# Partial sums of the up products held in PSUM, and the two plain down products of batches 2 to 7 split into quarters

## The chip, the cores and the metric

The kernel runs on one core of a Trainium2 chip. The metric is the device time of one execution in microseconds. TensorE (PE, with PEld for its weight loads) multiplies matrices, VectorE (DVE) does elementwise work, ScalarE (ACT) does activation functions and copies, and SyncE (SP) issues the transfers between the main memory and the on-chip memory. TensorE writes its results to PSUM, from where VectorE or ScalarE fetch them. All data here are 32-bit floats; a float32 matrix product of the program stands in the trace as two records of the same shape.

## What is computed

The reference, cut to what matters:

```python
# x: (8, 8, 512, 64), state: (8, 8, 32, 64)
a  = softmax(scale * x @ state.T);  xread = a  @ state
a2 = softmax(scale * state @ x.T);  sread = a2 @ x
rows = concat([xread, sread], axis=2)      # to (8 * 544, 512)
h = rows @ w_in                            # 512 -> 2048
g = h * (1.0 / (1.0 + exp(-1.702 * h)))
out = g @ w_out                            # 2048 -> 512
```

The 512 rows of x of each of the 8 batches go through both large products, and at the very end the 32 state rows of all batches together ("sr").

The kernel replaces the usual 8 products of 2x2 blocks by 7 (the Strassen-Winograd scheme): with A and B split into 2x2 blocks,

```
S1 = A21 + A22   S2 = S1 - A11   S3 = A11 - A21   S4 = A12 - S2
T1 = B12 - B11   T2 = B22 - T1   T3 = B22 - B12   T4 = B21 - T2
P1 = A11 B11  P2 = A12 B21  P3 = S4 B22  P4 = A22 T4  P5 = S1 T1  P6 = S2 T2  P7 = S3 T3
U2 = P1 + P6   C11 = P1 + P2   C12 = U2 + P5 + P3
C21 = U2 + P7 + P4             C22 = U2 + P7 + P5
```

(In the code the names of the parts are those of the kernel.)

## The kernel before

The first product ("up", rows @ w_in, with the softmax's product folded in) is done per block of features u, in seven products of 4 records each. PSUM banks hold x, y and z; VectorE adds what is in a bank to what it has already put into the on-chip memory (c21, c12, c22), and ScalarE takes the result through the activation function:

```python
def begin(u):
    nc.scalar.copy(c21, product(u, "x", l11, b11, True))
    add(product(u, "y", m2, t2, True), c21, c12)
def middle(u):
    z = product(u, "z", m1, t1, True)
    gelu(c11, product(u, "x", l12, b21, False))      # goes on summing in the bank
    add(product(u, "y", l21, t3, False), c21, c22)
    add(z, c22, c22)
    gelu(c22, c22)
def end(u):
    add(product(u, "y", l22, t4, False), c21, c21)
    gelu(c21, c21)
    add(product(u, "z", m4, b22, False), c12, c12)
    gelu(c12, c12)
    ...
    if u: s12(b, u - 1, ntok)                         # S1, S2 of the second product
for u in range(NU):                                   # NU = 4
    begin(u)
    if u: end(u - 1)
    middle(u)
    ...
def rest():
    end(NU - 1)
    s12(b, NU - 1, ntok)
    for u in range(NU): s3(b, u, ntok)
```

`add` is one VectorE instruction of 512 columns. `rest` runs inside the second product, after the first half of P1 ("P1a" below). The second product ("down", g @ w_out) is also done in seven products P1 to P7. Five of them (P3 to P7) are split again, into seven products of quarters, each of 8 records of 128x128. P1 and P2 are plain: 32 records each of 128x256:

```python
product(bank(0), A_of(0, 0), B11, "P1")
nc.scalar.copy(k1, bank(0))
...
sums_of((S1, r), (S2, (q1, q2, q4)))                  # sums for P5 and P6
third_of(S1)
product(bank(1), A_of(0, 1), B21, "P2")
tt(osb, bank(1), k1)
out(0, 0, osb)
hook("P2")
...                                                   # P5, P6, P3, P7, P4, each by strassen_low
```

The split form, with three banks x, y, z and `at(i)` for work of other parts that is put between the products:

```python
def strassen_low(left, right, bank, R, at):
    product(x, a11, b11, True);   nc.scalar.copy(p, x);    at(1)
    product(y, s2, t2, True);     add(u2, y, p);           at(2)
    product(x, a12, b21, False);  nc.scalar.copy(c11, x);  at(3)
    product(z, s1, t1, True);     add(c22, z, p);          at(4)
    product(y, a21, t3, False);   add(c22, y, c22);        at(5)
    product(z, s4, b22, False);   add(c12, z, u2);         at(6)
    product(y, a22, t4, False);   add(c21, y, p);          at(7)
```

(Summing goes on in one bank with `False`: after `u2` has been read, the fifth product lands on top of the second.) The sums s1, s2, s4 and the third (in place of a21) of the left side are made by VectorE before or during the product that stands ahead; those of the right side (t1, t2, t4) are kept outside and loaded, 768 KB each time (`low_load(k, i)`), into one of two places.

Attention work of the next batch hangs on named places in this sequence (`turn_x` ahead of the second product, then at "P1a" the state, at "P2a" the scores, the matrices M 0 and 1, and the maxima; later the exponentials, sums, transposes, and M 2 and 3). Each engine works through its own instructions strictly in the program's order (the program is scheduled by hand).

Of the kernel before, what the change touches and what calls it, by code (L numbers as in the profile page):

```python
# [10 lines left out]
FP32 = mybir.dt.float32  # L11
# [3 lines left out]
ALU = mybir.AluOpType  # L15
# [5 lines left out]
def kernel(  # L21
# [30 lines left out]
    nc = tc.nc  # L52
# [39 lines left out]
    def att_ps(shape, name):  # L92
        return psA.tile(shape, FP32, tag="att", name=name)
# [356 lines left out]

    def att_M(b, c, spare=False):

        m = mpool.tile([P, NG, FC], FP32, tag=f"M{turns['M'] % NFC if b < 2 else c}", name=f"M_{b}_{c}")
        turns["M"] += 1
        A[b]["M", c] = m
        name = f"M_{b}_{c}_"
        ps = [psH.tile([P, FC], FP32, tag="h", name=name + str(g)) if spare else att_ps([P, FC], name + str(g)) for g in range(NG)]
        by_state(b, ps, lambda rows, j: w_in[c][rows, j])
        for g in range(NG):
            nc.scalar.copy(m[:, g], ps[g])  # L460
# [177 lines left out]

    outside = {k: dram.tile([P, 3 * FC], FP32, name=f"low_{k}") for k in range(2, 7)}
    turn_rooms = [low[:, 3 * i : 3 * i + 3].rearrange("p k n -> p (k n)") for i in range(2)]  # L640
# [38 lines left out]

    def strassen_low(left, right, bank, R, at):  # L680

        b11, t3, b21, b22, t1, t2, t4 = right
        a11, a12, a21, a22, s1, s2, s4 = left
        p, u2 = (pu[:, i] for i in range(2))
        x, y, z = (v[:, :P] for v in bank)

        def product(ps, lhs, rhs, first):
            for f in range(QF):
                nc.tensor.matmul(  # L689
                    ps, lhs[f], rhs[:, f], start=(first and f == 0), stop=(f == QF - 1), skip_group_check=True  # L690
                )

        def add(out, x0, x1):
            nc.vector.tensor_tensor(out=out, in0=x0, in1=x1, op=ALU.add)

        c11, c12, c21, c22 = (R[:, i, P * k : P * (k + 1)] for i in range(2) for k in range(2))
        product(x, a11, b11, True)
        nc.scalar.copy(p, x)
        at(1)
        product(y, s2, t2, True)  # L700
        add(u2, y, p)
        at(2)
        product(x, a12, b21, False)
        nc.scalar.copy(c11, x)
        at(3)
        product(z, s1, t1, True)
        add(c22, z, p)
        at(4)
        product(y, a21, t3, False)
        add(c22, y, c22)  # L710
        at(5)
        product(z, s4, b22, False)
        add(c12, z, u2)
        at(6)
        product(y, a22, t4, False)
        add(c21, y, p)
        at(7)

    def strassen_two(key, dst, hooks, a4):
# [63 lines left out]

        product(bank(0), A_of(0, 0), B11, "P1")
        nc.scalar.copy(k1, bank(0))
        *r, p5 = spare_M()
        r = [v.rearrange("p (k h t) -> p k h t", k=2, h=2) for v in r]
        p5 = p5.rearrange("p (r n) -> p r n", r=2)
        sums_of((S1, r), (S2, (q1, q2, q4)))
        third_of(S1)  # L790
        product(bank(1), A_of(0, 1), B21, "P2")
        osb = opool.tile([P, 2, HN], FP32, tag="osb", name=f"osb_{key}_00")
        tt(osb, bank(1), k1)
        out(0, 0, osb)
# [20 lines left out]

        def sums(y, rooms):


            r1, r2, r4 = rooms

            def parts(k, i):
                return [y(2 * k + f // 2, i)[:, f % 2] for f in range(QF)]

            def both(fn):
                def step():
                    for u in range(NU // 2):
                        fn(u)

                return step

            return [
                both(lambda u: tt(r1[:, u], y(u, 1), y(2 + u, 1))),
                both(lambda u: tt(r2[:, u], r1[:, u], y(u, 0), ALU.subtract)),
                both(lambda u: tt(y(u, 1), y(u, 0), y(u, 1), ALU.subtract)),
                both(lambda u: tt(r4[:, u], y(2 + u, 0), r2[:, u], ALU.subtract)),
            ], (parts(0, 0), parts(1, 0), parts(0, 1), parts(1, 1), *(blocks(v) for v in rooms))

        def lowly(name, left, right, kept, banks, R, own):
            def at(i):
                for fn in own.get(i, ()):  # L840
                    fn()
                hook(f"{name}.{i}")

            b11, t3, b21, b22 = halves_of(right)
            strassen_low(left, (b11, t3, b21, b22, *kept), banks, R, at)

        def y_of(u0, o):
            return lambda u, i: g[u0 + u][:, :, o + P * i : o + P * (i + 1)]

        steps3, left3 = sums(y_of(0, half), (v1, v2, v4))  # L850
# [14 lines left out]
        lowly("P3", left12, B22, low_b, [h0, h1, o], p3, own3)  # L865
        if key + 1 < B:
            low_load(5, 1)
        hook("run")
# [5 lines left out]
        lowly("P7", left3, T3, low_a, [o, h0, h1], k3, {k + 1: steps4[k : k + 1] for k in range(4)})  # L874
        if key + 1 < B:
            low_load(2, 0)
        osb = opool.tile([P, 2, HN], FP32, tag="osb", name=f"osb_{key}_11")
# [16 lines left out]
    def hooks_next(b):  # L894
# [5 lines left out]

        at("P1a", att_state, b)
        at("P2a", att_scores, b)

        at("P2a", load_x, b)
        at("P2a", att_M, b, 0)
        at("P2a", att_M, b, 1, True)
        at("P2a", att_blocks, b)
        at("P2a", att_s_max, b)
        at("P2a", att_s_exp, b)
        at("P2a", eT_out, b)  # L910
        at("P2a", x_max, b, 0)
        at("P2a", x_sub, b, 0)
        at("P5.1", x_exp, b, 0)
# [117 lines left out]
    def up_strassen(b, ntok, left, right, between=(), beside=()):  # L1031
# [4 lines left out]
        b11, b21, b22, t1, t2, t3, t4 = right  # L1036
        banks = {}

        def product(u, bank, lhs, rhs, first):
            if first:  # L1040
                if bank == "x":
                    banks[bank, u] = psH.tile([P, 2, QT], FP32, tag="h", name=f"upx_{b}_{u}")
                else:
                    o = bank_o[2 * (u % 2) + (bank == "z")]
                    banks[bank, u] = o[:, : 2 * QT].rearrange("p (k t) -> p k t", k=2)
            ps = banks[bank, u]
            n = len(lhs)
            for k in range(2):
                o = 2 * P * (u % 2) + P * k
                for i in range(n):  # L1050
# [3 lines left out]
                    )  # L1054
            return ps

        def gelu(dst, src):
            nc.scalar.activation(out=dst, in_=src, func=AF.Gelu_apprx_sigmoid)  # L1058

        def add(ps, x, dst):  # L1060
            nc.vector.tensor_tensor(out=dst, in0=ps, in1=x, op=ALU.add)  # L1061

        def aside():
            if beside:
                fn, args = beside.pop(0)
                fn(*args)


        def begin(u):
            l11, l12, l21, l22, m1, m2, m4 = left(u)  # L1070
            G[b, u], G[b, NU + u] = free.pop(0), free.pop(0)
            _, c12 = quarters(b, u, ntok)
            c21, _ = quarters(b, NU + u, ntok)
            nc.scalar.copy(c21, product(u, "x", l11, b11, True))
            add(product(u, "y", m2, t2, True), c21, c12)
            aside()

        def middle(u):
            l11, l12, l21, l22, m1, m2, m4 = left(u)
            c11, c12 = quarters(b, u, ntok)  # L1080
            c21, c22 = quarters(b, NU + u, ntok)
            z = product(u, "z", m1, t1, True)
            gelu(c11, product(u, "x", l12, b21, False))
            add(product(u, "y", l21, t3, False), c21, c22)
            add(z, c22, c22)
            gelu(c22, c22)
            aside()

        def end(u):
            l11, l12, l21, l22, m1, m2, m4 = left(u)  # L1090
            c11, c12 = quarters(b, u, ntok)
            c21, c22 = quarters(b, NU + u, ntok)
            add(product(u, "y", l22, t4, False), c21, c21)
            gelu(c21, c21)
            add(product(u, "z", m4, b22, False), c12, c12)
            gelu(c12, c12)
            aside()
            if u:
                s12(b, u - 1, ntok)

        for u in range(NU):
            begin(u)
            if u:
                end(u - 1)
            middle(u)
            for fn, args in between[u] if u in between else ():
                fn(*args)

        def rest():
            end(NU - 1)  # L1110
            s12(b, NU - 1, ntok)
            for u in range(NU):
                s3(b, u, ntok)

# [153 lines left out]
    for b in range(1, B):  # L1268
        if b > 1:
            ahead = {"P1a": [(up_strassen(b, S, *parts_x(b), A[b]["sums"]), ())]}  # L1270
        else:
# [7 lines left out]
        else:  # L1279
# [6 lines left out]
            hooks["P3.7"] = [(low_third, (T1,))]  # L1286
            beside = steps[10:16] + [(low_third, (t,)) for t in (T2, T3, T4, B22)]
            ahead["P1a"][:0] = [steps[i] for i in (0, 1, 4, 5)]
        for name, first in ahead.items():
# [45 lines left out]
```

## Time and profile before

| | |
|---|---|
| time, median of three runs | 708.77 us (708.74 to 708.86) |
| span of the profiled execution | 706.9 us |
| ScalarE: copies out of PSUM on the line of `begin` (L1074), 512 columns | 24, mean 573 ns |
| ScalarE: activation on PSUM (L1058), 512 columns | 24, mean 597 ns |
| VectorE: s12's two lines (L565, L566), 512 columns | 28 each, mean 683 and 692 ns |
| VectorE: additions of 128 columns in the split products (L694), largest group | 42, mean 281 ns |
| share of the 16 transfer engines | 42.3% |
| loads of right-hand sums (low), 256 KB | 78, 3.8 us to landing |

The busy time of an engine counts the time in which at least one of its instructions is under way; instructions of one engine overlap a little, so a group's mean is longer than the distance from one start to the next. A line of the chain gives the start and the length of a piece of work that was on the path to the end. In the timeline, what stands in brackets is the idle time of that engine ahead of the instruction, and what ended it.

### The profile page before, as it was taken

The page shows a single profiled execution, that of the slowest core. Times are in us where ns is not written, and L with a number is a line of the kernel's source. Part 1 is how long each engine was busy: PE and PEld are TensorE (multiplying, and loading weights), DVE is VectorE, ACT ScalarE, POOL GpSimd, SP SyncE. Part 2 cuts the span into 40 slices and gives each one's busy share as a digit, 9 for nine tenths or more (in the row PEclk, how much of TensorE's full clock was granted, in tenths as well). Part 3 has the DMA queues.
Part 4 walks back from the last instruction along what each step waited for, and adds up shares of the span by engine and source line. Part 5 has one row for each costly group of instructions (what it writes and reads, how often), then busy time and mean ns, then how long its engine had stood idle before and what let it go on. Part 6 is the DMA issues. An engine that isn't in the chain of part 4 may idle for free.

```text
span 706.9 us, 12667 instructions
## 1 busy us (share of the span) xinstructions
PE 694.9 (98%) x4973; PEld 558.1 (79%) x4975; DVE 602.4 (85%) x1246; ACT 230.8 (33%) x456; POOL 0.8 (0%) x8
## 2 busy tenths in 40 slices
PE   8989999999999999999999999999999999999996
PEld 3433544458998799879988899889987998899995
DVE  6999799999978998799978996899789987888650
ACT  5686520014224413433243423342243124200210
POOL 0000000000000000000000000000000000000000
PEclk9999999999999999999999999999999999999999
DMA  8921246228742384309550765047432940041001
GB/s 230 368 74 54 93 146 154 115 89 206 213 118 37 61 194 145 69 9 206 148 105 1 152 182 120 16 82 199 137 51 48 194 148 16 0 125 57 16 1 29
DMA packets 143914, 77.89 MB, mean 110 GB/s; under 512 B 113904, under 2 KB 127728, under 8 KB 143856
## 3 DMA queue, kind: packets, MB, share of 16 engines
q1 hardware_dynamic: 143856, 77.09, 42.3%
q8 instruction: 39, 0.64, 0.4%
q14 instruction: 19, 0.16, 0.1%
HBM read 61.08 MB, written 15.99 MB: 109 GB/s over the span
## 4 chain that ended last, share of the span: by engine, by line
PE 95%; ACT 2%; DMA 2%; SPq 0%; DVE 0%; issue 0%; DVEq 0%
PE low L689 21%; PE o L1051 17%; PE o L738 14%; PE o L689 10%; PE o L542 8%; PE h L524 7%; PE upx L1051 6%; PE M L320 4%; PE o L585 2%; PE o L320 1%; PE sr L500 1%; PE warm L125 1%; PE upx_sr L1051 1%; DMA out_dram<-osb_sr 1%; DMA xn<-in_x_dram 1%; ACT low L219 1%
## 5 line engine op out<-in xcount | busy, mean ns | idle before, releaser
L1061 DVE TENSOR_TENSOR g<-o,g 128x512 f32<-128x512 f32 (+1 forms) x140 | 88.0, 650 | 51.1 <-PE o L1051 50.1
L738 PE MATMUL o<-w_out,g 128*128 128x256 f32 x448 | 100.6, 381 | 0.0
L738 PEld LDWEIGHTS o<-w_out,g 128*128 128x128 f32 x448 | 84.4, 190 | 16.6 <-issue 5.5
L1058 ACT ACTIVATE g<-g 128x512 f32<-128x512 f32 (+1 forms) x84 | 49.8, 600 | 100.9 <-DVE g L1061 100.9
L1051 PE MATMUL upx<-aT,M 128*128 128x256 f32 x192 | 49.3, 379 | 0.0
L1051 PE MATMUL o<-ta,M 128*128 128x256 f32 x192 | 49.3, 379 | 0.0
L1051 PE MATMUL o<-ta,ms 128*128 128x256 f32 x192 | 48.3, 379 | 0.0
L689 PE MATMUL low<-low,g 128*128 128x128 f32 x336 | 44.4, 275 | 0.0
L689 PEld LDWEIGHTS low<-low,g 128*128 128x128 f32 x336 | 40.9, 192 | 0.0
L460 ACT COPY M<-M 128x512 f32<-128x512 f32 x64 | 33.1, 598 | 22.7 <-PE M L320 22.7
L1051 PEld LDWEIGHTS o<-ta,ms 128*128 128x128 f32 x192 | 36.6, 190 | 4.9
L1051 PEld LDWEIGHTS o<-ta,M 128*128 128x128 f32 x192 | 36.6, 190 | 4.9
L1051 PEld LDWEIGHTS upx<-aT,M 128*128 128x128 f32 x192 | 36.1, 191 | 4.6
L689 PE MATMUL low<-sums,later 128*128 128x128 f32 x280 | 37.0, 275 | 0.0
L689 PEld LDWEIGHTS low<-sums,later 128*128 128x128 f32 x280 | 34.6, 192 | 0.4
L320 PE MATMUL M<-w_in,stT 64*32 64x512 f32 x512 | 31.9, 594 | 0.0
L527 ACT ACTIVATE g<-h 128x512 f32<-128x512 f32 x24 | 14.0, 591 | 54.7 <-PE h L524 54.7
L524 PE MATMUL h<-low,M 128*128 128x512 f32 x64 | 29.6, 597 | 1.5 <-DVE low L408 1.5
L524 PE MATMUL h<-aT,M 128*128 128x512 f32 x64 | 28.7, 599 | 1.4 <-ACT M L460 1.4
L689 PE MATMUL low<-w_out,g 128*128 128x128 f32 x224 | 29.6, 275 | 0.0
L542 PE MATMUL o<-w_out,g 128*128 128x512 f32 x64 | 28.6, 594 | 0.0
L542 PE MATMUL o<-w_out,sums 128*128 128x512 f32 x64 | 28.3, 593 | 0.0
(210 smaller groups left out, 1295.2 us busy)
## 6 DMA issues: line engine op xcount, KB each, us to landing
low<-low SPq DMA_DIRECT2D x78, 256.0 KB, 3.8
later<-in_moe_w_out_dram SPq DMA_DIRECT2D x16, 512.0 KB, 3.6
xn<-in_x_dram SPq DMA_DIRECT2D x28, 256.0 KB, 4.8
low<-low SPq DMA_DIRECT2D x9, 768.0 KB, 4.0
w_out<-in_moe_w_in_dram SPq DMA_DIRECT2D x12, 512.0 KB
xsq<-in_x_dram SPq DMA_DIRECT2D x96, 64.0 KB, 2.3
out_dram<-osb SPq DMA_DIRECT2D x18, 256.0 KB, 3.1
out_dram<-later SPq DMA_DIRECT2D x14, 256.0 KB, 2.2
```

What stands on the lines that cost most here:

```text
L125: nc.tensor.matmul(ps, zeros[:, :P], zeros, start=True, stop=True)
L320: nc.tensor.matmul(ps[g][st], A[b]["stT"][rows, st], rhs(rows, j), start=True, stop=True)
L460: nc.scalar.copy(m[:, g], ps[g])
L524: nc.tensor.matmul(hps, lhs[i], rhs[i], start=(i == 0), stop=(i == n - 1))
L527: nc.scalar.activation(out=G[key, f // 2][:, f % 2, :ntok], in_=hps, func=AF.Gelu_apprx_sigmoid)
L542: nc.tensor.matmul(ops, G[key, f // 2][:, f % 2, P * r : P * (r + 1)], w_out[:, f], start=(f == 0), stop=(f == NF - 1))
L585: nc.tensor.matmul(ps[:, r], lhs[f][:, P * r : P * (r + 1)], rhs[:, f], start=(first and r == 0 and f == 0), stop=(f == HF - 1), skip_grou ...
L689: nc.tensor.matmul(ps, lhs[f], rhs[:, f], start=(first and f == 0), stop=(f == QF - 1), skip_group_check=True)
L738: nc.tensor.matmul(ps[:, r], lhs[f][:, P * r : P * (r + 1)], rhs[:, f], start=(r == 0 and f == 0), stop=(f == HF - 1), skip_group_check=True,)
L1051: nc.tensor.matmul(ps[:, k], lhs[i][:, o : o + P], rhs[i], start=(first and k == 0 and i == 0), stop=(i == n - 1), skip_group_check=True,)
L1058: nc.scalar.activation(out=dst, in_=src, func=AF.Gelu_apprx_sigmoid)
L1061: nc.vector.tensor_tensor(out=dst, in0=ps, in1=x, op=ALU.add)
```

## The change

It has two parts. First, the sums of the up products are left in PSUM: ScalarE copies the first product x into the bank y beforehand (a seed), so that the next products sum on top of it, and one of the two other sums is written by VectorE into a bank z, on which again a product sums. VectorE then adds twice in each u, where it added five times; ScalarE copies three times, where it copied once. The activation reads the banks. `s12` and `s3` of the block before are done among the up products. Second, P1 and P2 of the batches 2 to 7 become seven products of quarters too, as P3 to P7 are; batch 1 keeps the plain ones. The aim is less work on TensorE (7 of 8 quarter products in P1 and P2), with room on VectorE made by the first part. For it the right-hand sums of B11 and B21 are made in batch 1 and kept outside, and two more loads take place in each batch. What hung on "P1a" and "P2a" moves.

The core of the diff, with cuts marked:

```diff
@@ strassen_low
-        product(x, a11, b11, True)
...
+        def q1(): product(x, a11, b11, True);   nc.scalar.copy(p, x)
+        def q2(): product(x, a12, b21, False);  nc.scalar.copy(c11, x)
+        def q6(): product(y, s2, t2, True);     add(u2, y, p)
+        def q5(): product(z, s1, t1, True);     add(c22, z, p)
+        def q7(): product(y, a21, t3, False);   add(c22, y, c22)
+        def q3(): product(z, s4, b22, False);   add(c12, z, u2)
+        def q4(): product(y, a22, t4, False);   add(c21, y, p)
+        for i, q in enumerate((q1, q5, q2, q6, q7, q3, q4) if late else (q1, q6, q2, q5, q7, q3, q4)):
+            q()
+            at(i + 1)
@@ strassen_two
-        product(bank(0), A_of(0, 0), B11, "P1")
-        nc.scalar.copy(k1, bank(0))
+        if key == 1:
+            product(bank(0), A_of(0, 0), B11, "P1")
+            nc.scalar.copy(k1, bank(0))
+        else:
...
+            for fn in steps1:                      # 8 instructions of 256 columns
+                fn()
+            o, h0, h1 = low_banks()
+            lowly("P1", left1, B11, low_b, [h0, o, h1], p1, {}, True)
+            nc.scalar.copy(k1, p1)
+            low_load(5, 1)
...
+            for fn in steps2:                      # 8 more
+                fn()
+            hook("P1")
...
-        sums_of((S1, r), (S2, (q1, q2, q4)))
-        third_of(S1)
-        product(bank(1), A_of(0, 1), B21, "P2")
-        tt(osb, bank(1), k1)
+        if key == 1:
...
+        else:
+            o, h0, h1 = low_banks()
+            own2 = {2: [lambda: sums_of((S1, r))], 4: [lambda: third_of(S1)], 5: [lambda: sums_of((S2, (q1, q2, q4)))]}
+            lowly("P2", left2, B21, low_a, [h0, o, h1], osb, own2, True)
+            low_load(2, 0)
+            tt(osb, osb, k1)
@@ strassen_two, after P3 (and alike after P7, with B21 and place 0)
-        if key + 1 < B:
-            low_load(5, 1)
+        if key == 1:
+            low_made(0, B11, 1)
+            low_third(B11)
+        elif key + 1 < B:
+            low_load(0, 1)
@@ hooks_next
+        p1, p2 = ("P1a", "P2a") if first else ("P1.2", "P1")
+        at(p1, att_state, b)
+        at(p2, att_scores, b)
...
+        at("P2a" if first else "P2", x_max, b, 0)
+        at("P2a" if first else "P2", x_sub, b, 0)
@@ up_strassen
+        first_x(0); seed(0); first_w(0)            # seed: nc.scalar.copy(Y(u), X[u])
+        for u in range(NU):
...
+            if u + 1 < NU: first_x(u + 1)
+            product(Y(u), u, m2, t2)
+            nc.scalar.copy(c12, Y(u))
+            add(Z(u), W[u], c12)
+            aside()
+            if u: last_y(u - 1)                    # product(Y, l22, t4), gelu
+            if u + 1 < NU: seed(u + 1)
+            product(X[u], u, l12, b21)
+            gelu(c11, X[u])
+            if u: sums_after(u - 1)                # s12, s3
+            product(Y(u), u, l21, t3)
+            nc.scalar.copy(c22, Y(u))
+            add(c22, W[u], c22)
+            gelu(c22, c22)
+            aside()
+            if u + 1 < NU: first_w(u + 1)
+            product(Z(u), u, m4, b22)
+            gelu(c12, Z(u))
...
+        def rest():
+            last_y(NU - 1)
+            sums_after(NU - 1)
@@ the loop over the batches
-            ahead = {"P1a": [(up_strassen(b, S, *parts_x(b), A[b]["sums"]), ())]}
+            ahead = {"P1.1": [(up_strassen(b, S, *parts_x(b), A[b]["sums"]), ())]}
...
-            beside = steps[10:16] + [(low_third, (t,)) for t in (T2, T3, T4, B22)]
+            beside = steps[10:16] + [(low_third, (t,)) for t in (B11, B21, T2, T3, T4, B22)]
-            ahead["P1a"][:0] = [steps[i] for i in (0, 1, 4, 5)]
+            ahead["P1.2"] = [steps[i] for i in (0, 1, 4, 5)]
```

## The prediction

> **What bounds the kernel now.** I read the page first (busy time and chain), then one batch cut out of the steady part by its period, then the timeline of that batch, which gives the cost of single instructions. The page:
>
> ```profile
> PE 694.9 (98%) x4973; PEld 558.1 (79%) x4975; DVE 602.4 (85%) x1246; ACT 230.8 (33%) x456; POOL 0.8 (0%) x8
> ...
> PE 95%; ACT 2%; DMA 2%; SPq 0%; DVE 0%; issue 0%; DVEq 0%
> ...
> L1061 DVE TENSOR_TENSOR g<-o,g 128x512 f32<-128x512 f32 (+1 forms) x140 | 88.0, 650 | 51.1 <-PE o L1051 50.1
> L738 PE MATMUL o<-w_out,g 128*128 128x256 f32 x448 | 100.6, 381 | 0.0
> ```
>
> TensorE sets the end: 95% of the chain. But VectorE, at 85%, has little to spare, and an average hides where. The chain in order of time repeats every 75.63 us (281.08, 356.71, 432.34, always the first up product of a batch). So I cut the batch 356.71 to 432.34 into stretches; the columns are length, then busy time of PE, PEld, DVE, ACT, POOL, then granted clock, DMA share and GB/s:
>
> ```profile
> 356.71:380.00 23.29, 23.29 (x109) 20.55 (x109) 17.34 (x28) 11.45 (x19) 0.00 (x0) 1.00 0.32 60
> 380.00:392.20 12.20, 12.20 (x89) 9.54 (x94) 11.46 (x20) 2.41 (x5) 0.00 (x0) 1.00 0.00 0
> 392.20:397.00 4.80, 4.80 (x43) 3.56 (x28) 4.70 (x11) 4.51 (x8) 0.00 (x0) 1.00 1.02 198
> 397.00:410.00 13.00, 13.00 (x118) 13.00 (x118) 12.61 (x34) 2.49 (x8) 0.00 (x0) 1.00 0.91 187
> 410.00:421.00 11.00, 11.00 (x168) 9.50 (x168) 10.93 (x30) 3.49 (x10) 0.00 (x0) 1.00 0.63 200
> 421.00:432.34 11.34, 11.34 (x99) 11.24 (x99) 9.37 (x24) 0.85 (x4) 0.00 (x0) 1.00 0.41 117
> ```
>
> See two things. TensorE has no gap anywhere. VectorE is idle for 6 us in the first stretch (the up products) and for 2 us in the last; from 380 to 421 it works 39.7 of 41 us. TensorE runs just ahead of a VectorE that is full there.
>
> The cost of one instruction must be its start-to-start distance, not its "mean ns", which overlaps with its neighbour. From the timeline:
>
> ```profile
> 355.68 1.03 PE L1051 MATMUL upx<-aT,M 128*128 128x256 f32 x4
> ...
> 356.74 0.58 ACT L1074 COPY g<-upx 128x512 f32<-128x512 f32 x1 [4.17 <-PE upx L1051]
> ...
> 379.66 2.48 DVE L156 STREAM_TRANSPOSE xsq<-xsq 128x512 f32<-128x512 f32 x4
> ...
> 389.18 0.69 DVE L745 TENSOR_TENSOR spare_M<-later 128x512 f32<-128x512 f32 x1
> 389.78 0.68 DVE L745 TENSOR_TENSOR g<-later 128x512 f32<-128x512 f32 x1
> ...
> 398.50 1.06 PE L689 MATMUL low<-sums,later 128*128 128x128 f32 x8
> 398.77 0.29 DVE L694 TENSOR_TENSOR pu<-low,pu 128x128 f32<-128x128 f32 x1
> 398.98 0.68 DVE L745 TENSOR_TENSOR g<-g,later 128x512 f32<-128x512 f32 x1
> ...
> 416.00 0.75 DVE L745 TENSOR_TENSOR later<-g,g 128x256 f32<-128x256 f32 x2
> 416.67 0.75 DVE L745 TENSOR_TENSOR later<-later,g 128x256 f32<-128x256 f32 x2
> ```
>
> VectorE: 0.60 us for 512 columns (389.18 to 389.78; about 0.71 where it needs the result just before it), 0.335 for 256 (two in 0.67), 0.20 for 128. TensorE: an up product of 4 records takes 0.862 (16 such records of 128x256 on L738 take 3.45 us in the chain), a quarter product of 8 records 0.894. From the start of an up product to the ScalarE copy that reads it: 1.06 us, so 0.20 after the next product has begun. A copy of 512 columns is done after 0.58.
>
> [...] a product that accumulates onto a bank waits until VectorE has read it; in the built program each such matmul waits for a VectorE semaphore. No line of the trace before shows that wait lasting, since it is always met there.
>
> **The change part by part.**
> TensorE: P1 and P2 of batches 2 to 7 were 64 records by 0.2156 = 13.80 us a batch; they become 14 quarter products by 0.894 = 12.52. Saved 1.29 us a batch, 7.7 in six.
> VectorE, up products: five additions per u become two; 12 fewer in a batch, by 0.60 = 7.2 us less. ScalarE gets 8 more copies, about 4.6 us, of a time in which it is half idle.
> VectorE, P1 and P2: each gets 8 sums of 256 columns (2.68) and 5 additions (1.0), together 7.4 us more.
> So VectorE's total hardly changes. But the 7.2 leave the stretch where it was idle, and the 7.4 enter the stretch where it was full. In exchange seven instructions of the late part go: two additions of the last up products, and s12 of one u and s3 of three, now done among the up products; 7 x 0.60 = 4.2 us. Some 3.2 us net are added where VectorE was full, and the dependences make it worse. I walk through one batch (2 to 6), t = 0 at the first up product, in the order in which the built program has each engine's instructions:
>
> - Up: 27 products, then the first product of P1 at 23.3. By the walk no wait: the copies between two products of one bank are ready 0.1 us or more ahead.
> - The last c22 is copied after the product that ends at 22.43: 22.64 + 0.58 = 23.2; its addition to 23.9. Then VectorE turns x of the next batch, 4 x 0.60: to 26.25. Only then the first sum of P1: both halves done at 27.0.
> - TensorE has nothing but P1's first product (to 24.2) and the last up product (to 25.05). The second product of P1 needs that sum: it starts near 26.7. **Wait 1.7.**
> - VectorE: sums to 28.9, s12 and s3 of the last u to 30.9, then P1's two additions, done 31.35. The fifth product accumulates onto the bank that the second of them reads, and stands straight after the product that filled it. TensorE is there at 29.6: **wait 1.8.**
> - The additions of P1's last three products each follow TensorE, so VectorE is mostly idle until 34.5. Then P2's sums (2.7), two transposes and the maxima of the scores (2.8), one addition, three sums for P5 (2.0): P2's like addition is done at 42.5. TensorE has the scores, M and four products, to 40.4: **wait 2.1.**
> - In P5 the same pattern behind x_max, x_sub and s4: **0.45 and 0.6.** In P6 VectorE is just in time again.
>
> Sum 6.6, less 1.3: a batch longer by 5.3 us; five batches 26.6. Batch 7 turns no x, but its four sums for the state rows stand between P1's additions: waits 3.7 and 2.0, less 1.3, 4.4. Batch 1 keeps its plain products and makes the sums of B11 and B21: 8 instructions by 0.62, 5 us in a VectorE that was full (410 to 421 in its own batch's copy), less the 1.6 us that it idles in P4: about 3. The third sums undone before the state rows cost 2 x 0.6 where VectorE has room. 708.8 + 26.6 + 4.4 + 3 = 742.8.
>
> **The rivals.**
> (1) TensorE stays the only bound: 708.8 - 7.7 = 701. For it: TensorE's share and the unchanged VectorE total. Against: 380 to 421 above. A version of it with only the unavoidable gap (product, addition, next product on one bank, some 0.6 us in P1 and in P2 each) would be 708.8 - 7.7 + 7 = 708.
> (2) ScalarE's new copies stop TensorE among the up products: 8 hand-offs a batch, the tightest about 0.1 us early. If each lost 0.2 us: 1.6 a batch, 10 us in all; alone 711, with my waits 750. Against: ScalarE has 11.5 busy of 23.3 us there.
> (3) A transfer is late: two more loads of 768 KB in a batch, and P5's and P6's sums are now loaded after P1 and P2, where the DMA share is 0.91 to 1.02. By the walk they have 8 us and more, and pieces of 256 KB land in 3.8. Late by 1 us a batch it would add 6.
>
> **Range and chances.** The waits come from orders that are fixed and durations that repeat, so their sign is fairly sure; each is good to some 0.3 us, five of them in six batches to some 9 us all the same way. If half of them were hidden by something I overlooked, 725; with rivals 2 or 3 on top, 755. Slower by over 2% means over 723. Predicted 743, range 727 to 755; faster by over 2% 0.01 (even rival 1 gives 1.1%), within 2% 0.09, slower 0.90.
>
> **What would show it.** Right: the batch takes near 81 us; TensorE's waits are for VectorE on the quarter products of P1 and P2, and gone from P6 on; the stretch of the up products has none; VectorE idles about 3 us in the second half of P1. Wrong: a period near 74.3 (rival 1), TensorE waits for ScalarE at up products (2) or for a load (3), or sums of 256 columns much under 0.33 us.

## The result, and the profile after

The changed kernel takes 757.98 us (median; 756.88 to 760.5), the kernel before 708.77: a ratio of 1.070, 95% interval 1.068 to 1.072. Predicted were 743, range 727 to 755. The direction and the kind of cost were right; the size was 15 us short.

The page of the changed kernel, the same lines as before (busy time by engine, the granted clock in 40 slices, the chain by engine):

```profile
PE 705.7 (93%) x5261; PEld 569.3 (75%) x5263; DVE 603.7 (80%) x1328; ACT 263.6 (35%) x536; POOL 0.8 (0%) x8
...
PEclk9999999999999999999999999999999999899999
...
PE 69%; DVE 17%; ACT 6%; DMA 3%; issue 3%; SPq 0%; DVEq 0%; ACTq 0%
```

VectorE's busy time has hardly moved (602.4 to 603.7), as worked out. Yet the chain, 95% TensorE before, now runs through VectorE for 17% and through ScalarE for 6%. So the same amount of VectorE's work stands at worse places. PE's busy time has gone up (694.9 to 705.7) although there is less to multiply: in part because some products ran at a lower clock (0.50 in the stretches shown below), which the slice with an 8 in the row of the clock hints at (c1 below, whose clock drops only at the very end, has 697.5).

TensorE's waits in the whole span (total, times, longest):

```profile
PE o L691 <- DVE pu L696: 15.6, 12, 3.5
PE low L691 <- ACT pu L702: 11.2, 5, 2.2
```

The first line was predicted. The second, five waits of 2.2 us for a ScalarE copy, was not. One batch, which begins at 457.19 and lasts 82.71 us (75.63 before), shows where both stand. From TensorE's timeline (start, length; in brackets the idle time and what ended it):

```profile
484.09 1.13 PE L691 MATMUL low<-low,spare_M 128*128 128x128 f32 x8 [1.53 <-issue]
...
488.72 1.16 PE L691 MATMUL o<-w_out,g 128*128 128x128 f32 x8 [1.61 <-DVE pu L696]
...
498.65 1.16 PE L691 MATMUL low<-w_out,g 128*128 128x128 f32 x8 [2.25 <-ACT pu L702]
...
501.23 1.16 PE L691 MATMUL o<-w_out,left 128*128 128x128 f32 x8 [0.53 <-DVE pu L696]
...
508.14 1.16 PE L691 MATMUL low<-sums,later 128*128 128x128 f32 x8 [0.17 <-DVE pu L696]
509.67 1.16 PE L691 MATMUL o<-sums,spare_M 128*128 128x128 f32 x8 [0.37 <-DVE spare_M L696]
```

The lines are P1's second and fifth product, P2's third and fifth, and two of P5. Besides the wait, see the length: a quarter product right after a wait shows 1.13 to 1.16, most others 1.06. It ends up to 0.1 us later; with the six waits here and smaller ones not shown, that is some 0.9 us in a batch more than before.

For P1's second product this profile names no releaser (`issue`). VectorE's timeline has the turn of x, and behind it the sum that the product multiplies, up to the moment when it starts; in the profile of a4 below, where the same five waits occur, they are put down to that line:

```profile
481.20 2.48 DVE L156 STREAM_TRANSPOSE xsq<-xsq 128x512 f32<-128x512 f32 x4
483.61 0.71 DVE L758 TENSOR_TENSOR spare_M<-g,g 128x256 f32<-128x256 f32 x2
...
PE low L691 <- DVE spare_M L758: 7.9, 5, 1.6
```

Why P2's third product waits for ScalarE is in ScalarE's own timeline:

```profile
495.07 0.62 ACT L462 COPY M<-o 128x512 f32<-128x512 f32 x1
495.70 1.28 ACT L372 ACT_TABLE_LOAD   x1
497.00 0.69 ACT L372 ACTIVATE e<-o,mx 128x512 f32<-128x512 f32 x1
...
497.68 0.68 ACT L372 ACTIVATE e<-o,mx 128x512 f32<-128x512 f32 x1
...
498.34 0.26 ACT L702 COPY pu<-low 128x128 f32<-128x128 f32 x1
```

P2's third product accumulates onto the bank of its first, and must wait until ScalarE has copied that first product out. TensorE finished it near 495.3; but ScalarE has its instructions in order, and ahead of the copy stand the last copy of M, a table load of 1.28 us and the two exponentials of the scores. The copy runs 3 us late. (The first exponential starts 0.02 us after the end of the load, at 497.00 after 496.98.)

Last, the clock. Stretches of 3.41 us (length, busy time of PE, PEld, DVE, ACT, POOL, granted clock, DMA share, GB/s), two pairs with a drop and, between them, the two stretches over which P2's wait of 2.25 us in the batch at 457.19 is spread:

```profile
329.93:333.34 3.41, 1.34 (x12) 1.34 (x13) 2.15 (x6) 2.15 (x7) 0.00 (x0) 1.00 0.90 144
333.34:336.75 3.41, 3.03 (x15) 2.73 (x14) 1.84 (x4) 0.12 (x1) 0.00 (x0) 0.50 0.96 142
...
493.77:497.18 3.41, 2.63 (x32) 1.89 (x16) 3.38 (x8) 3.38 (x6) 0.00 (x0) 1.00 1.06 213
497.18:500.59 3.41, 1.94 (x16) 1.86 (x16) 2.12 (x6) 1.69 (x6) 0.00 (x0) 1.00 0.86 139
...
579.10:582.51 3.41, 1.17 (x11) 1.15 (x11) 2.12 (x7) 2.19 (x6) 0.00 (x0) 1.00 0.90 167
582.51:585.92 3.41, 3.03 (x15) 2.73 (x14) 2.03 (x4) 0.27 (x1) 0.00 (x0) 0.50 0.96 143
```

After P2's wait in the batches at 290.54 and 539.90 the granted clock is 0.50 for 3.41 us, and those two batches take 83.94 us where the other three take 82.71. In the last batch three such stretches are at 0.50, two of them in a row (654.2 to 661.0, and 667.9 to 671.3).

### The profile page after: what moved, and what is told of

The parts are those of the page before. It is cut to its first block, busy times and chain, and to the rows that moved or that the text cites. A ratio compares the mean times of both kernels' runs of the same rounds, so it can differ in the third digit from the quotient of the medians.

```text
span 757.2 us, 13522 instructions
## 1 busy us (share of the span) xinstructions
PE 705.7 (93%) x5261; PEld 569.3 (75%) x5263; DVE 603.7 (80%) x1328; ACT 263.6 (35%) x536; POOL 0.8 (0%) x8
## 4 chain that ended last, share of the span: by engine, by line
PE 69%; DVE 17%; ACT 6%; DMA 3%; issue 3%; SPq 0%; DVEq 0%; ACTq 0%
PE low L691 16%; PE o L691 11%; PE o L1113 11%; PE o L544 7%; PE h L526 7%; PE upx L1113 5%; DVE g L758 3%; PE M L320 3%; DVE spare_M L758 3%; PE o L587 2%; PE upw L1113 2%; DVE xsq L156 2%; ACT M L462 1%; ACT e L372 1%; DMA out_dram<-osb 1%
## 5 line engine op out<-in xcount | busy, mean ns | idle before, releaser
L691 PE MATMUL low<-w_out,g 128*128 128x128 f32 x416 | 56.2, 278 | 12.2 <-ACT pu L702 11.2
L691 PEld LDWEIGHTS low<-w_out,g 128*128 128x128 f32 x416 | 51.3, 192 | 17.8 <-ACT pu L702 12.2
L702 ACT COPY pu<-low 128x128 f32<-128x128 f32 x33 | 8.7, 264 | 97.7 <-PE low L691 65.2
L462 ACT COPY M<-M 128x512 f32<-128x512 f32 x59 | 30.7, 595 | 14.4 <-PE M L320 14.4
L1119 ACT ACTIVATE g<-o 128x512 f32<-128x512 f32 (+1 forms) x56 | 31.3, 559 | 10.7 <-PE o L1113 10.7
L691 PE MATMUL o<-w_out,g 128*128 128x128 f32 x160 | 23.3, 290 | 11.5 <-DVE pu L696 11.5
L691 PEld LDWEIGHTS o<-w_out,g 128*128 128x128 f32 x160 | 20.2, 198 | 17.7 <-DVE pu L696 12.6
L1122 DVE TENSOR_TENSOR o<-upw,g 128x512 f32<-128x512 f32 x18 | 12.6, 700 | 24.0 <-ACT g L1159 24.0
L1113 PE MATMUL o<-ta,ms 128*128 128x256 f32 x120 | 30.8, 379 | 0.0
L691 PE MATMUL low<-low,spare_M 128*128 128x128 f32 x160 | 22.0, 280 | 7.7 <-issue 6.1
```

The lines of the kernel that those rows point to most:

```text
L691: nc.tensor.matmul(ps, lhs[f], rhs[:, f], start=(first and f == 0), stop=(f == QF - 1), skip_group_check=True)
L1113: nc.tensor.matmul(ps[:, k], lhs[i][:, o : o + P], rhs[i], start=(first and k == 0 and i == 0), stop=(i == n - 1), skip_group_check=True,)
L1122: nc.vector.tensor_tensor(out=out, in0=ps, in1=x, op=ALU.add)
```

## The experiments

All times are medians; ratios are to the kernel before on the same chip (708.8).

**a1, part 1 alone.** The sums of the up products in PSUM, with P1 and P2 left as they were.

```diff
-            ahead = {"P1.1": [(up_strassen(b, S, *parts_x(b), A[b]["sums"]), ())]}
+            ahead = {"P1a": [(up_strassen(b, S, *parts_x(b), A[b]["sums"]), ())]}
...
-        if key == 1:
+        if True:
...
```

(`if key == 1` kept the plain P1 and P2 to batch 1.)

> Only the first part of the change: sums of the up products in PSUM; P1 and P2 stay plain in all batches, with no extra loads. Theory (the wait is made by VectorE's full queue in P1 and P2): 706 to 710 us, no wait of TensorE among the up products, VectorE about 7 us a batch lighter. Rival (the hand-offs through seeded banks stop TensorE): over 715 us, with waits of TensorE for ScalarE on the up products.

Measured: 709.55, ratio 1.0010 (1.0003 to 1.0017). VectorE's busy time falls from 602.4 to 551.3 and ScalarE's rises from 230.8 to 257.7, and nothing comes of it: TensorE was the bound among the up products before and still is. Rival 2 of the prediction (hand-offs from ScalarE stop the up products) falls.

**a2, part 2 alone.** The quarters in P1 and P2, with the old up products. The third sums of P1 overwrite blocks that the old order reads later, so other numbers come out; the instructions are the same.

```diff
-    def up_strassen(...):   # the changed one
+    def up_strassen(...):   # that of the kernel before
```

> Only the second part: the up products as before (five additions a u on VectorE, s12 and s3 late), P1 and P2 of batches 2 to 7 in quarters. Theory: the 7.4 us of VectorE's work a batch enter the full stretch without the 4.2 us that the first part takes out of it, so it is slower still than the change: 775 to 790 us. Rival (the first part is what hurts): 701 to 715 us.

Measured: 792.04, ratio 1.117 (1.115 to 1.120), 2 us above the range. P1's fifth product alone waits 5.9 us in a batch, and runs at half the clock afterwards (0.50 from 507.54 to 514.36 us; 2.08 instead of 1.06 to 1.16):

```profile
510.63 2.08 PE L691 MATMUL o<-w_out,g 128*128 128x128 f32 x8 [5.93 <-DVE pu L696]
```

So part 1 is what makes room for part 2: worth nothing alone, it takes 34 us off what part 2 costs. The room does not suffice.

**a3, without the sums of the left operands.** The 16 sums a batch that P1 and P2 need are left out and raw blocks multiplied in their place; the output is another.

```diff
-            for fn in steps1:
-                fn()
...
+            left1 = raw(y_of(0, 0))
...
-            for fn in steps2:
-                fn()
+            left2 = raw(y_of(NU, 0))
```

> The change with the 16 sums of 256 columns a batch left out (the products of P1 and P2 read the plain quarters in their place, so this part of the computation is missing), all products and their additions kept. Theory: 5.4 us less on VectorE in the full stretch; waits of about 0.9, 1.0 and 0.5 us stay, and the granted clock stays at 1.00: 718 to 730 us. Rival 1 (waits between adjacent products of one bank): 745 or more. Rival 2 (late loads): 755 or more, unchanged.

Measured: 741.52, ratio 1.046 (1.044 to 1.048): above the range by 11. P1's first wait is gone, but P2's third product waits for ScalarE exactly as long as before (2.25), and the clock drops to 0.50 after it in three of the five batches instead of two:

```profile
488.22 1.67 PE L691 MATMUL low<-w_out,g 128*128 128x128 f32 x8 [2.25 <-ACT pu L702]
489.69 1.91 PE L691 MATMUL o<-low,g 128*128 128x128 f32 x8
```

With 32 us less of VectorE's busy time this wait has not moved: that fits ScalarE's order, as the timeline above suggested; b2 below changes this order itself.

**a4, without the two added loads.** Two loads of right operands a batch are left out; the output is another.

```diff
-        elif key + 1 < B:
-            low_load(0, 1)
...
-        elif key + 1 < B:
-            low_load(1, 0)
```

> The change with the two additional loads of right-hand sums left out in batches 2 to 6 (P1 and P2 then multiply by sums of other products that lie there, so the values are others; the instructions of the engines are the same). Theory: 755 to 760 us, unchanged. Rival (transfers come late or crowd): at least 6 us less.

Measured: 756.54, ratio 1.067 (1.065 to 1.070). A batch without a drop of the clock takes 82.70 (82.71 with the loads), so the loads cost nothing that shows; the 1.4 us lie within the spread of the executions. Rival 3 falls.

**b1, the turn of x among the up products.**

```diff
-            if b > 1:
-                turn_x(b + 1)
...
-            ahead = {"P1.1": [(up_strassen(b, S, *parts_x(b), A[b]["sums"]), ())]}
+            ahead = {"P1.1": [(up_strassen(b, S, *parts_x(b), {**A[b]["sums"], **({2: [(turn_x, (b + 1,))]} if b + 1 < B else {})}), ())]}
```

> The changed kernel, with the turn of x of the next batch (4 x 0.60 us of VectorE) moved from P1's first product to the up products, where VectorE has about 1.95 us of slack in each batch. Theory (VectorE's order: at P1 the turn stands ahead of the sum that TensorE waits for): the two waits of P1, 1.7 and 1.8 us together, shrink to about 1.0, so about 2.45 us in each of five batches, some 12 in all: 740 to 748. Rival (VectorE has as much work as before, so the wait only moves to a later product or into the up products): 756 to 760.

Measured: 751.11, ratio 1.059 (1.057 to 1.061); outside the range, though P1 did what the theory said: the wait before its second product is gone, the one before its fifth is 1.49 (product to product). A batch without a drop of the clock now takes 80.65, some 2.06 less than 82.71; five of those are 10 us. But there is just one such batch; in the next four P2's wait falls so that the clock drops each time, and they take 82.01 to 82.23:

```profile
406.82:410.23 3.41, 1.17 (x10) 0.98 (x10) 2.15 (x7) 3.05 (x7) 0.00 (x0) 1.00 1.26 218
410.23:413.64 3.41, 3.29 (x16) 2.99 (x15) 2.06 (x4) 0.27 (x1) 0.00 (x0) 0.50 0.73 109
488.74:492.15 3.41, 1.17 (x10) 0.97 (x10) 2.15 (x6) 3.15 (x7) 0.00 (x0) 1.00 1.25 225
492.15:495.56 3.41, 3.41 (x16) 3.17 (x16) 2.07 (x4) 0.27 (x1) 0.00 (x0) 0.50 0.74 111
```

81.92 us lie between the two drops, 24 times 3.413, as between any two neighbours of the four from 328.31 to 574.07 us: the batch has come into step with the points at which the clock drops, and so meets one each time.

**b2, the exponentials behind P2's first copy.**

```diff
-        at(p2, att_s_exp, b)
-        at(p2, eT_out, b)
+        at("P2a" if first else "P2.1", att_s_exp, b)
+        at("P2a" if first else "P2.1", eT_out, b)
```

> The changed kernel, with the two exponentials of the scores (and the turn of their results that follows) moved behind ScalarE's first copy of P2. Theory (P2's third product waits for that copy because the table load and the exponentials stand ahead of it in ScalarE's order): the wait of 2.4 us there goes, and P2's fifth product, then bound by VectorE alone, starts some 1.2 us earlier in each of five batches; with less of the clock's drop that follows the long wait: 746 to 754. Rival (VectorE sets P2's end whatever ScalarE does, as the prediction had it): 756 to 760.

Measured: 749.33, ratio 1.057 (1.056 to 1.059). The five waits for ScalarE are gone. VectorE's wait before P2's fifth product is longer (1.77 instead of 0.53) but that product starts 1.27 us earlier in the batch; each of the five batches takes 81.45, and none has a drop of the clock:

```profile
492.18 1.06 PE L691 MATMUL o<-low,left 128*128 128x128 f32 x8
495.01 1.16 PE L691 MATMUL o<-w_out,left 128*128 128x128 f32 x8 [1.77 <-DVE pu L696]
```

So the two waits in P2 overlap: VectorE's alone is 1.9 (495.01 less 492.18 and 0.894), near the 2.1 of the prediction; ScalarE's, which it lacked, adds 1.2 on top.

**b3, the waits filled.** Products of the identity with itself, read by nobody, ahead of each of the four products that wait in P1 and P2.

```diff
+            fill(i + 1)
             q()
...
+    FILL = {('P1', 2): (6, 0), ('P1', 5): (7, 14), ('P2', 3): (9, 0), ('P2', 5): (2, 8)}
```

(In brackets on the right: how many, in batches 2 to 6 and in the last.)

> The changed kernel, with products of 128 x 128 of the identity with itself, whose sums nobody reads, put into TensorE's order ahead of the products that wait: 6 and 7 (14 in the last batch) in P1, 9 and 2 (8 in the last batch) in P2. They fill the waits and take none away. Theory (the clock falls to half because TensorE stood idle; that costs some 7 us in the whole span): the granted clock stays at 1.00, 750 to 754. Rival (the clock falls for another cause, or the fillers delay as much as they save): 757 or more.

Measured: 752.72, ratio 1.062 (1.061 to 1.064). All five batches take 82.7, the clock falls nowhere inside the kernel (only after its last product), and from the last batch's start to the end are 129.4 us instead of 133.4. Additional work made the kernel 5.3 us faster; nothing else was changed, so the drops come from TensorE's idleness and cost at least that much.

**b4, four orders changed together.** b1 and b2, with the last s12 and s3 and batch 7's row sums among P1's later products.

```diff
...
+            ahead = {"P1.1": [(rest_up, ())], "P1.5": [(late_sums, ())]}
...
+            ahead["P1.6"] = ahead.get("P1.6", []) + [steps[i] for i in (0, 1, 4, 5)]
```

> The changed kernel with the turn of x among the up products, the exponentials behind P2's first copy, and the second and third sums of the last row block, and in batch 7 the last row sums, moved to P1's later products. Theory (the cost is in the order of VectorE's and ScalarE's work around two products, and only the rest in its amount): waits of about 0.6, 2.2 and 0.9 us are left in a batch, the batch takes about 78.7 us, 726 to 738. Rival (the amount of VectorE's work in the quarters sets it, whatever the order): 750 to 758.

Measured: 736.85, ratio 1.040 (1.038 to 1.042). No instruction less than in the changed kernel, 21 us faster. A wait of 2.3 for VectorE is left at P2's fifth product, and a drop to 0.50 after it in three of five batches.

**c1, half of P2's left sums among P1's products.**

```diff
+            ownp = {3: [rooms2, half2(0), half2(1)], 4: [half2(2), half2(3)]}
+            lowly("P1", left1, B11, low_b, [h0, o, h1], p1, ownp, True)
...
-            for fn in steps2:
-                fn()
+            for fn in later2["steps"]:
+                fn([1])
```

> The order of b4, and further: half of P2's left sums (row blocks 0 and 2 of the lower half, four sums of 0.335 us) among P1's products, where VectorE idles 0.9 and 1.25 us; the turn of x one row block earlier; in batch 7 the last row sums behind P2's fourth product. Theory (the order around two products, and the clock's drop after them, is what is left of the cost): P2's wait of 2.3 us shrinks to about 1.0 and gives no drop of the clock, batch 7 has neither its wait of 2.8 us nor its drop: some 2 us less in each of five batches and 4 in the last: 721 to 729. Rival (from P1 to P6 VectorE has no idle left to give, so the wait only moves to P5 and P6): 733 to 737.

Measured: 725.91 (725.80 to 725.92), ratio 1.024 (1.022 to 1.026). All waits of a batch that are left:

```profile
469.79 1.16 PE L691 MATMUL o<-w_out,g 128*128 128x128 f32 x8 [0.38 <-DVE pu L696]
...
480.36 1.16 PE L691 MATMUL o<-w_out,left 128*128 128x128 f32 x8 [1.10 <-DVE pu L696]
...
487.27 1.16 PE L691 MATMUL low<-sums,later 128*128 128x128 f32 x8 [0.17 <-DVE pu L696]
488.80 1.16 PE L691 MATMUL o<-sums,spare_M 128*128 128x128 f32 x8 [0.37 <-DVE spare_M L696]
```

A batch takes 77.78 us, still 2.15 more than before: waits of 2.68 from product to product, 0.76 of restarts, less the 1.29 saved. No drop of the clock is left inside.

**c2, P5's sums later.**

```diff
-            own2 = {2: [lambda: sums_of((S1, r))], 4: [lambda: third_of(S1)], 5: [lambda: sums_of((S2, (q1, q2, q4)))]}
+            own2 = {4: [lambda: sums_of((S1, r))], 5: [lambda: third_of(S1)], 6: [lambda: sums_of((S2, (q1, q2, q4)))]}
```

> c1, and P5's left sums behind P2's fourth to sixth product instead of its second to fifth, so that P2's fourth sum, which the fifth product waits for, does not stand behind three sums of 0.7 us. Theory: the rest of P2's wait goes, and a smaller one comes at P5, some 0.5 us less in each batch: 717 to 727, but not below the 708.8 of the kernel before. Rival (P5 waits for what was moved, as long as P2 did): as c1 or above it.

Measured: 730.82, ratio 1.031 (1.029 to 1.032), 5 us above c1 and so as the rival had it. P2's fifth product waits 0.38 instead of 1.10, but at P2's seventh and in P5 there are now waits of 0.2, 0.48 and 0.49 (the 0.48 is for a ScalarE copy that has itself waited for VectorE's last addition of P2), and the batch is 0.6 longer than in c1: what is moved is missed a few products later. In the last batch P2's seventh product waits 2.61 instead of 1.16. This fits the amount of VectorE's work as what is left, no longer its order: in c1 VectorE works 21.86 of the 23.65 us from 465.62, where P1's sums begin, to 489.27. But only this one further order was tried, so it is argued and not shown. No version here is faster than the kernel before.

## Why the prediction missed, point by point

- *TensorE saves 1.29 us a batch, VectorE's total hardly changes, its work moves to where it was full*: right (page, a1, a2).
- *Among the up products no wait*: right (a1: none).
- *P1: waits of 1.7 and 1.8*: measured from product to product 1.70 and 1.77. Right, and so are their causes: b1 takes the first away with the turn of x, and b4, which also moves the last s12 and s3, leaves 0.38 us of idle time at the second. (That the fifth product has to wait for VectorE at all lies in the program: it adds onto a sum that has still to be read.)
- *P2: "TensorE has the scores, M and four products, to 40.4: wait 2.1"*: here the step failed. TensorE does not get through the four products: the third waits 2.44 for ScalarE, then the fifth 0.69, together 3.1. The walk had VectorE's and TensorE's order in P2 but not ScalarE's, and looked for ScalarE only among the up products (rival 2). b2 shows 1.9 for VectorE alone, and without the wait for ScalarE it takes 749.33, inside the range.
- *The clock*: the sum has no term for it; the walk gives each product its full-speed length, also after a wait. In the profiled execution it falls to 0.50 behind waits in two of the five batches and in the last. b3, which fills the waits, takes 752.72, inside the range too: with either of the two overlooked terms taken away the time lies in it (b2's five batches have no drop left either).
- *P5: 0.45 and 0.6; P6 none*: 0.34 and 0.54, and none. Right.
- *Sum 6.6 a batch*: 7.5 of waits and 0.9 that the walk did not have at all (mostly the 0.1 us of each restart), less 1.29, so that the batch is longer by 7.08 instead of 5.3: 8.9 us in five batches.
- *Batch 7: waits 3.7 and 2.0, so 4.4*: the waits were 3.68 and 1.98, but from its first up product to the end 9.0 us were added. About 4.0 of the 4.6 in excess are the clock: with the same waits but no drop, this stretch is 129.3 us in a4's profile, and 129.4 in b3's with the waits filled, instead of 133.4. P1's fifth to seventh products took 1.71 to 1.86 us each instead of 0.894 to 0.99. The remaining 0.6 was not traced.
- *Batch 1: 3*: 3.4.
- *The cuts at 281.08, 356.71 and 432.34, "always the first up product"*: each is 1.03 us behind that product's start, as the prediction's own line at 355.68 shows. The period of 75.63 stands all the same.

So the miss of the profiled execution, 758.99 against 742.8, is 8.9 (P2's wait for ScalarE and the restarts), 2 x 1.23 and 4.6 (the clock in two batches, and mostly the clock in the last) and 0.4 (batch 1), which makes 16.4 where 16.2 were measured. Of the 8.9, P2's wait for ScalarE makes some 6 (1.26 a batch between the changed kernel and b2) and the restarts 4.5; waits a little shorter than predicted give the rest back. Rival 1 falls with the result: its batch would have taken near 74.3. "Each wait good to 0.3 us" was true of the waits that had been found; the range was too narrow for one overlooked and for what a wait does to the products behind it.

Of the 49 us that the change costs, the orders changed in b4 and c1, with the drops that went with them, are 32. The 17 that remain are 5 x 2.15 in the batches, 3.4 in batch 1 and 3.0 in the last.

## What to carry to other kernels

When work is given to an engine, walk through the order of every engine that hands something back in that stretch, also one that is 35% busy: what counts is what stands ahead of the hand-back in its queue, here a table load and two exponentials. A total that does not change says nothing; the same work of VectorE and ScalarE cost 757.98 or 725.91 us by its order alone, the clock's drops included, and a part that brings nothing by itself (a1) can be what another part lives on. And look at the clock behind each long wait of TensorE: here one of 2.25 us was followed by a granted clock of 0.50 in two batches of five, and these took 1.23 us more.

## What the runs showed of the hardware

In these profiles the drops of the granted clock begin whole multiples of 3.413 us apart, a step that the batch does not set. In the changed kernel they begin at 333.34, 582.51, 654.20 and 667.85 us: 73, 21 and 4 such steps apart, where a batch without a drop takes 82.71 us, 24.2 steps. In b1 they begin at 328.31, 410.23, 492.15, 574.07, 649.16 and 659.40 us: 24, 24, 24, 22 and 3 steps apart. In the ten profiles cut into such steps (the changed kernel, a1 to a4, b1 to b4 and c1, from 70 us after the start), each step at full clock in which TensorE was busy for 1.44 us or less was followed by one at 0.50, apart from one near the end of c1 (at 717.01, busy 1.43 us). After a step with 1.64 or more none was at 0.50; in between, 1.49 to 1.60, both occur. Where a wait of some 2.3 us was spread over two steps, it thus cost only itself, and where it lay in one, 1.2 to 1.6 us more (batches without and with a drop: 82.71 and 83.94 in the changed kernel, 80.02 and 81.25 to 81.50 in a3, 82.70 and 83.92 to 83.94 in a4, 80.65 and 82.01 to 82.23 in b1; in b4, where it was less, 79.00 to 79.34 and 79.64 to 79.96). A longer wait went free as well: in a4's last batch one of 3.52 us is spread so that no step has less than 1.54 of work, and no drop follows. And in a2 each batch, of some 88.8 us, meets a drop, and the first five of these begin 88.75 us (26 steps) apart.

This fits that repeated executions of kernels with drops in only some batches spread (756.88 to 760.5; b1 748.35 to 751.86) and those of c1, without any inside, hardly (725.80 to 725.92). The mean granted clock of each execution goes along: in the changed kernel 0.986 at 760.5, 0.988 at 758.99, and 0.992 and 0.993 at 756.96 and 756.88. Since only one execution of each was profiled, that the spread comes from where the batches fall among these steps is argued and not shown.
